# A new order table for a fused recurrence and feed-forward kernel

## The chip, the cores and the metric

The kernel runs on one core of a Trainium2 chip. The time is device microseconds of one execution; a profiled execution gives the trace. Engines are named as in the profile: PE (matmul), PEld (its weight loads), DVE (vector), ACT (activations), POOL, and SP, which here only issues DMAs.

## The reference

Four batches, eight heads, 768 steps, head size 48. A gated linear recurrence with a complex decay gives y, which is laid out as rows of 8 x 48 = 384 numbers; a layer norm and a two-layer network (384 to 1536 to 384) follow, with a residual.

```python
mag = np.sqrt(a_re * a_re + a_im * a_im)
scale = np.minimum(mag, 0.999) / (mag + 1e-06)
...
for t in range(S):
    new_re = ar * S_re - ai * S_im
    new_im = ar * S_im + ai * S_re
    kv = np.einsum('bhd,bhe->bhde', k[:, :, t], v[:, :, t])
    S_re, S_im = (new_re + kv, new_im)
    y[:, :, t] = np.einsum('bhd,bhde->bhe', q[:, :, t], S_re)
...
xn = (x - mu) / np.sqrt(var + 1e-06) * g_ln
ch = np.maximum(xn @ w_ch1, 0.0) @ w_ch2
return (x + ch).astype(np.float32)
```

## The kernel before

The 4 x 768 rows are 24 chunks of 128 steps, n = 0 to 23, taken as 12 pairs, P = 0 to 11 (three pairs in a batch). The recurrence is done chunk by chunk as masked attention: with cumulated log decays and phases, q and k are scaled so that a product of the two gives the weights inside a chunk, and a carried state G (384 numbers on each partition) brings in the past.

Every piece of work is an operation with a name. `name.P` and `name.P.i` belong to a pair, `name.n` to a chunk. Pair 0 is cut in two halves by heads (`.0.0` and `.0.1`), the others are whole. In the order of a pair:

- Inputs, by SP: `are`, `aim` (384 KB a pair, halves of 192 KB in pair 0), `k`, `q`, `vf` (192 KB a chunk).
- The decay: `ln`, `iv` (ACT), `r` = aim/are, `r2` = its square, `u` = log(1 + r2) (ACT), `l` and `lc` (DVE): the capped log of the magnitude. `dec` (PE) cumulates it with a triangular matrix, `e` and `en` (ACT) are its exponentials.
- The phase: `th` (arctangent, ACT), `ph` (PE) cumulates it, `car` carries its end to the next pair, `sin` and `cos` (ACT). In pairs 0 to 3 a small matmul `qt` adds a quarter turn in PSUM ahead of `cos`; it waits for `sin` and `car`. Later pairs take `abs` and a bias.
- `ke`, `qe` = k, q times the exponentials, `ks`, `qs` = those times cos and sin, on DVE or POOL. `v` is a cast of `vf`.
- Transposes: `kT`, `qT` on PE (eight 128-wide ones each) with the copies `ksT`, `qsT` on ACT or DVE, or `ksT`, `qsT` as a DMA transpose on SP, with no PE work.
- Attention: `am` (PE), `atm` (mask, DVE), `y` (PE, from `atm`, `v`, `qsT` and the state), `x` (copy). State: `gm` (PE), `G` (copy, or product with `decc`, which comes from `dps`).
- Network: `bn`, `rstd` (statistics), `xtr`, `xT` (x transposed), `mm1` (six groups of six matmuls a pair, three of `relu`), `mm2` (three groups of four a chunk), `ot` (scaling by rstd and residual; some are split into `oa` on ACT and `ot` on POOL), `st` (store, SP).

The layer norm's gain and mean are folded into w1 once: `wl.0` (POOL) loads w1 by DMA with a cast, `wp.0` to `wp.2` (PE) form its weighted column means, nine `wc` (DVE) subtract them; `mm1.P.g` needs `wc.g.*`. `wl.1` loads w2, which `mm2` needs.

Nothing is scheduled by the compiler. `PLAN` is a list of `name:engine`, with the PSUM bank behind the letter (`P0` is PE into bank 0, `A2` ACT reading bank 2), and its order is the order on each engine; `@other` makes the operation wait for another one too. An engine goes strictly through its list and waits for semaphores of others. Buffers are rings (`RINGS`); the order must respect them. Two kinds of entries compute nothing: `tab.log` and `tab.trig` (ACT) load the table of logarithm and exponential, or of sine and arctangent, ahead of their use; `warm` (PE) are fillers, matmuls whose result is not read, to keep TensorE busy while it would wait.

Of the kernel before, what the change touches and what calls it, by code (L numbers as in the profile page):

```python
# [806 lines left out]
```

## Time and profile before

| What | before |
|---|---|
| median of 3 runs | 193.94 us (193.87 to 194.18) |
| profiled execution | span 191.74 us, 193.94 us with what lies around the span |
| PE busy | 175.3 us (91%) |
| ACT busy | 165.2 us (86%) |
| DVE busy | 154.8 us (81%) |
| POOL busy | 109.2 us (57%) |
| table loads, fillers | 23, 74 |
| loads and stores | 37.56 MB, 196 GB/s over the span |

A busy share is an average over stages: in the first 37 us the engines wait for each other and for the inputs, later several are full at once. The page's fourth part, the chain, follows the end of the program back through what released each step. A matmul's duration in the trace includes its way through the array, which overlaps the next ones; what it costs in a dense run is the distance between starts.

### The profile page before, as it was taken

Reading aid. Unit: us, or ns where it says so; the run is one execution under the profiler, and the core shown is the slowest. Engines: PE = TensorE matmul, PEld = TensorE weight load, DVE = VectorE, ACT = ScalarE, POOL = GpSimd, SP = SyncE. Lnnn points to the kernel's source line nnn. Section 1 sums busy time; section 2 is a strip of 40 time slices with the busy share of each in tenths; the row PEclk is TensorE's granted clock in tenths of the full one; section 3 lists DMA queues with packets and bytes.
Section 4 is the critical chain, followed back from the end, with each engine's and each line's share of the span. In section 5 each row is a group of like instructions: output and inputs, shape, how many; then the busy total and the mean of one; then the engine's idle time right before and its main releaser. Section 6 shows DMA issues by size and latency. Waiting matters only on the chain.

```text
span 191.7 us, 5125 instructions
## 1 busy us (share of the span) xinstructions
PE 175.3 (91%) x2039; PEld 132.7 (69%) x2039; DVE 154.8 (81%) x267; ACT 165.2 (86%) x234; POOL 109.2 (57%) x124
## 2 busy tenths in 40 slices
PE   5567958999999989999999999999999999999991
PEld 3355644577786777787686877868777678787760
DVE  2369996999999998799999989997987484868612
ACT  3999999989999999999799988999999989427540
POOL 8601449927695599652496764585495857600500
PEclk9999996999999999999999999999999999999997
DMA  6999999999899979999899996999998979996033
GB/s 151 291 244 219 236 190 203 168 218 298 184 212 237 166 163 255 192 258 211 161 169 265 167 255 152 184 288 253 204 228 153 208 145 144 248 103 165 3 129 118
DMA packets 132104, 37.56 MB, mean 196 GB/s; under 512 B 127088, under 2 KB 131696, under 8 KB 132080
## 3 DMA queue, kind: packets, MB, share of 16 engines
q1 hardware_dynamic: 130128, 34.88, 87.7%
q0 software_dynamic: 1952, 2.36, 7.3%
q8 instruction: 16, 0.26, 0.5%
q14 instruction: 8, 0.07, 0.1%
HBM read 28.31 MB, written 4.72 MB: 172 GB/s over the span
## 4 chain that ended last, share of the span: by engine, by line
PE 38%; ACT 27%; DVE 16%; issue 8%; DMA 4%; POOL 3%; SPq 1%; DVEq 0%; POOLq 0%; ACTq 0%
PE banks L741 14%; PE banks L720 9%; ACT h L731 5%; ACT L775 4%; DVE w1b L388 3%; DMA qsT<-qs 3%; PE banks L477 2%; PE banks L616 2%; DVE l L466 2%; ACT r L462 2%; ACT en L481 2%; PE banks L496 2%; PE banks L593 2%; ACT r L458 2%; DMA are<-in_a_re_dram 2%
## 5 line engine op out<-in xcount | busy, mean ns | idle before, releaser
L741 PE MATMUL banks<-w2b,h 128*128 128x384 bf16 x288 | 54.9, 326 | 0.3 <-ACT h L731 0.2
L720 PE MATMUL banks<-xT,w1b 128*128 128x256 bf16 x432 | 51.9, 272 | 0.8 <-ACT trig L514 0.5
L720 PEld LDWEIGHTS <-w1b 128*128 128x128 bf16 x432 | 41.2, 98 | 7.7 <-DVE xT L291 1.3
L741 PEld LDWEIGHTS <-h 128*128 128x128 bf16 x288 | 26.0, 97 | 14.3 <-ACT h L731 0.8
L294 DVE TENSOR_TENSOR atm<-banks,mask 128x1024 bf16<-128x1024 f32 x24 | 28.7, 1217 | 5.2 <-PE banks L616 2.8
L731 ACT ACTIVATE h<-banks 128x1024 bf16<-128x1024 f32 x24 | 24.1, 1023 | 8.7 <-PE banks L720 8.5
L775 ACT ACT_TABLE_LOAD x23 | 29.5, 1283 | 1.2 <-PEq L791 0.8
L294 POOL TENSOR_TENSOR ks<-ke,trig 128x768 bf16<-128x768 bf16 x14 | 22.8, 1640 | 8.8 <-DVE ke L294 2.8
L294 POOL TENSOR_TENSOR qs<-qe,trig 128x768 bf16<-128x768 bf16 x11 | 18.0, 1641 | 12.3 <-DVE ot L755 5.0
L294 POOL TENSOR_TENSOR ke<-k,en 128x384 bf16<-128x384 f32 x18 | 16.5, 930 | 11.8 <-DMA vf<-in_v_dram 10.3
L294 POOL TENSOR_TENSOR qe<-q,e 128x384 bf16<-128x384 f32 x16 | 14.6, 921 | 12.2 <-ACT e L481 5.9
L733 DVE TENSOR_SCALAR h<-banks 128x1024 bf16<-128x1024 f32 x12 | 14.5, 1215 | 4.9 <-PE banks L720 4.9
L753 POOL TENSOR_TENSOR ot<-ot,x 128x384 f32<-128x384 f32 x8 | 7.3, 916 | 14.6 <-ACT ot L746 13.6
L616 PE MATMUL banks<-qsT,ksT 128*128 128x128 bf16 x192 | 14.3, 219 | 1.4 <-DVE ksT L291 1.2
L616 PEld LDWEIGHTS <-ksT 128*128 128x128 bf16 x192 | 12.1, 98 | 3.4 <-DVE ksT L291 1.4
L496 PE MATMUL banks<-th,u_th 128*128 128x384 f16 (+1 forms) x52 | 12.4, 325 | 2.2 <-ACT th L485 2.2
L679 DVE BATCH_NORM_STATS2 stats<-x 128x6 f32<-128x384 bf16 x24 | 13.1, 547 | 0.0
L755 DVE SCALAR_TENSOR_TENSOR ot<-banks,rstd,x 128x384 f32<-128x384 f32 x16 | 9.6, 609 | 4.1 <-DMA out_dram<-ot 2.9
L466 DVE SCALAR_TENSOR_TENSOR l<-r,w 128x768 f16<-128x768 f16 (+1 forms) x13 | 11.5, 892 | 1.6 <-ACT r L462 1.6
L770 PE MATMUL banks<-u_e 128*128 128x256 f16 x74 | 10.5, 302 | 2.2 <-POOL u_e L328 2.2
L477 PE MATMUL banks<-l,u_e 128*128 128x384 f16 (+1 forms) x52 | 10.4, 327 | 2.2 <-DVE l L469 1.3
L448 ACT ACTIVATE w<-are 128x768 f32<-128x768 f32 (+1 forms) x13 | 10.3, 796 | 2.2 <-DMA are<-in_a_re_dram 2.2
(96 smaller groups left out, 372.1 us busy)
## 6 DMA issues: line engine op xcount, KB each, us to landing
q<-in_q_dram SPq DMA_DIRECT2D x24, 192.0 KB, 4.0
k<-in_k_dram SPq DMA_DIRECT2D x24, 192.0 KB, 4.1
vf<-in_v_dram SPq DMA_DIRECT2D x24, 192.0 KB, 4.2
...
w2b<-in_moe_w_ch_dram POOLq DMA_DIRECT2D x1, 1152.0 KB, 11.9
```

The costliest lines, as they stand in the source:

```text
L294: {"DVE": nc.vector, "POOL": nc.gpsimd}[eng(name)].tensor_tensor(**kw)
L466: nc.vector.scalar_tensor_tensor(out=S_("l"), in0=S_("r2"), scalar=0.5, in1=S_("w"), op0=ALU.mult, op1=ALU.add)
L477: nc.tensor.matmul(heads(ps[:, c]), lhsT=u_e[:, c, j], rhs=step(T("l", P), j), start=(j == 0), stop=(j == R - 1))
L496: nc.tensor.matmul(heads(ps[:, c]), lhsT=u_th[:, c, j], rhs=step(T("th", P), j), start=False, stop=(j == R - 1), skip_group_check=True)
L616: nc.tensor.matmul(ps[:, h], lhsT=T("ksT", n)[:, h], rhs=T("qsT", n)[:, h], start=True, stop=True)
L679: nc.vector.bn_stats(out=T("stats", n), in_=T("x", n))
L720: nc.tensor.matmul(ps[:, jj], lhsT=w1b[:, dc, ts(gi * JG + jj, C)], rhs=T("xT", P)[:, dc].rearrange("p c t -> p (c t)"), start=(dc == 0), ...
L731: act(out=dst, in_=src, func=AF.Relu)
L733: nc.vector.tensor_scalar(out=dst, in0=src, scalar1=0.0, scalar2=None, op0=ALU.max)
L741: nc.tensor.matmul(bank(f"o.{n}")[:, 0:DM], lhsT=T("h", P)[:, j, ts(c, C)], rhs=w2b[:, j], start=(j == 0), stop=(j == NJ - 1))
L770: g.add(f"warm.{i}", lambda i=i: nc.tensor.matmul(bank(f"warm.{i}")[:, 0:256], lhsT=u_e[:, 0, 0], rhs=u_e[:, 1].rearrange("p j t -> p (j t ...
L775: g.add(f"tab.{nm}.{i}", lambda tab=tab: nc.scalar.preload_act_table_set(tab))
```

## The change

The whole order table is replaced, and the loop that declares fillers goes from 240 to 61. The operations that compute are the same; what differs is order, engine and bank, and which transposes are done by DMA. Counts in the table:

| kind | before | after |
|---|---|---|
| table loads (ACT) | 23 | 17 |
| fillers (PE) | 74 | 61 |
| kT and qT (PE) | 10 + 13 | 14 + 11 |
| ksT and qsT by DMA (SP) | 14 + 11 | 10 + 13 |
| ksT, qsT copies on ACT / DVE | 6 / 17 | 5 / 20 |
| ks, qs on POOL / DVE | 25 / 27 | 21 / 31 |
| ke, qe on POOL / DVE | 34 / 14 | 34 / 14 |
| xT on ACT / DVE | 11 / 13 | 7 / 17 |
| relu on ACT / DVE | 24 / 12 | 26 / 10 |
| G on ACT / DVE | 6 / 14 | 9 / 11 |
| r2 on ACT / DVE / POOL | 8 / 4 / 1 | 6 / 7 / 0 |
| v on ACT / DVE / POOL | 3 / 1 / 8 | 5 / 2 / 5 |
| rstd on ACT / POOL | 7 / 5 | 4 / 8 |

Up to the first mm1 the new table has 6 table loads, the old one 8. w1's load (`wl.0`) stood on POOL behind `v.0`; it now stands behind the constants and waits for `lc.0.1` on DVE. The inputs of pairs 0 and 1 come in another order on SP, `aim` first and `vf` last; pair 1's operations stand beside pair 0's, and pair 1's attention (`am.2`, `am.3`) ahead of the first mm1. The diff, cut to both tables' openings and ends:

```diff
@@ the order table @@
 PLAN = """
-are.1.0:S tab.log.0:A ln.1.0:A iv.1.0:A ue:G car0.1:G pad.ks.2:G zdec:G ident:G pad.ks.1:G pad.qs.0:G
-are.0.0:S gln:S are.0.1:S qrow:G car0.0:G pad.ks.0:G pad.qs.1:G ln.0.0:A pick:G iv.0.0:A ln.0.1:A aim.0.1:S
-aim.0.0:S uth:V iv.0.1:A r.0.1:V tab.trig.0:A th.0.1:A aim.1.0:S are.2.0:S q.0.0:S aim.2.0:S k.0.0:S q.2.1:S
-q.0.1:S k.0.1:S warm.0:P1 warm.1:P1 warm.2:P1 warm.3:P1 warm.4:P1 warm.5:P1 warm.6:P1 warm.7:P1 warm.8:P1
-warm.9:P1 warm.10:P1 warm.11:P1 warm.12:P1 warm.13:P1 warm.14:P1 warm.15:P1 warm.16:P1 warm.17:P1 warm.18:P1
-warm.19:P1 warm.20:P1 warm.21:P1 warm.22:P1 warm.23:P1 warm.24:P1 warm.25:P1 warm.26:P1 warm.27:P1
-warm.28:P1 ph.0.1:P0 q.1.0:S vf.0.1:S k.1.1:S r.0.0:V r2.0.0:A th.0.0:A one:G cmean:G wgc:V vf.0.0:S
-are.3.0:S sin.0.1:A0 k.1.0:S aim.3.0:S r2.0.1:V r.1.0:V r2.1.0:V tab.log.1:A u.0.0:A l.0.0:V u.0.1:A l.0.1:V
-lc.0.0:V warm.29:P2 warm.30:P2 warm.31:P2 warm.32:P2 warm.33:P2 warm.34:P2 warm.35:P2 warm.36:P2 warm.37:P2
-warm.38:P2 warm.39:P2 warm.40:P2 warm.41:P2 warm.42:P2 warm.43:P2 warm.44:P2 warm.45:P2 warm.46:P2
-warm.47:P2 warm.48:P2 warm.49:P2 warm.50:P2 warm.51:P2 dec.0.0:P1 u.1.0:A ln.2.0:A iv.2.0:A en.0.0:A1
-lc.0.1:V l.1.0:V dec.0.1:P2 ph.0.0:P3 car.0.1:V0 en.0.1:A2 e.0.1:A2 e.0.0:A1 lc.1.0:V r.2.0:V car.0.0:V3
-tab.trig.1:A sin.0.0:A3 qe.0.1.0:V qe.0.0.0:V q.1.1:S mask:G ke.0.0.0:G@qe.0.0.0 ke.0.1.0:V r2.2.0:V
-qs.0.0.1:V qs.0.1.1:V th.1.0:A qt.0.1:P0 warm.52:P4 warm.53:P4 warm.54:P4 warm.55:P4 warm.56:P4 warm.57:P4
-warm.58:P4 warm.59:P4 warm.60:P4 warm.61:P4 warm.62:P4 warm.63:P4 warm.64:P4 warm.65:P4 warm.66:P4
-warm.67:P4 warm.68:P4 warm.69:P4 qt.0.0:P3 dps.0:P2 cos.0.0:A3 cos.0.1:A0 ks.0.0.1:V ks.0.0.0:V ks.0.1.0:V
-qs.0.1.0:V ph.1.0:P4 dec.1.0:P6 qs.0.0.0:V warm.70:P1 warm.71:P1 qT.1:P3 tab.log.2:A en.1.0:A6 u.2.0:A
-ln.3.0:A iv.3.0:A e.1.0:A6 v.0:G@qs.0.0.0 decc.0:V2 ks.0.1.1:V vf.1.1:S vf.1.0:S q.2.0:S car.1.0:V4
-warm.72:P1 warm.73:P1 kT.0:P2 qT.0:P1 kT.1:P0 qsT.1:V3 tab.trig.2:A sin.1.0:A4 ksT.0:V2 wl.0:G ksT.1:V0
-am.1:P2 gm.0:P0 ke.1.0.1:G@ks.0.1.1 ke.1.0.0:G th.2.0:A qsT.0:V1 am.0:P6 dps.1:P1 decc.1:A1 qt.1.0:P4
-l.2.0:V r.3.0:V lc.2.0:V G.0:V0 gm.1:P0 cos.1.0:A4 dec.2.0:P4 k.2.1:S tab.log.3:A e.2.0:A4 en.2.0:A4
-atm.0:V6 atm.1:V2 G.1:V0 r2.3.0:V k.2.0:S are.4.0:S ph.2.0:P6 y.1:P1 aim.4.0:S ks.1.0.1:G@lc.2.0 x.1:V1
-are.5.0:S ks.1.0.0:G y.0:P2 kT.3:P3 x.0:V2 ksT.3:V3 u.3.0:A tab.trig.3:A sin.2.0:A6 wp.2:P0 wc.2.1:V0
-wc.2.0:V0 xtr.0:P1 wl.1:G xtr.1:P4 wp.0:P5 wp.1:P2 wc.2.2:V0 xT.1:V4 qt.2.0:P6 xT.0:A1 kT.2:P3 th.3.0:A
-cos.2.0:A6 wc.0.2:V5 wc.0.1:V5 wc.1.2:V2 wc.0.0:V5 wc.1.1:V2 ksT.2:A3 mm1.0.2.1:P0 mm1.0.2.0:P0
-qe.1.0.0:G@r2.3.0 qe.1.0.1:G qs.1.0.0:G relu.0.2:A0 ph.3.0:P6 qs.1.0.1:G qe.2.0.1:G qT.2:P3 qT.3:P4
-car.3.0:A6 mm1.0.0.1:P0 mm1.0.0.0:P0 wc.1.0:V2 qsT.3:V4 sin.3.0:A6 qt.3.0:P6 qsT.2:A3 mm1.0.1.0:P4 l.3.0:V
-lc.3.0:V qe.2.0.0:V aim.5.0:S v.1:G pad.qs.2:G am.3:P2 mm1.0.1.1:P4 cos.3.0:A6 bn.0:V bn.1:V relu.0.0:A0
-qs.2.0.0:G@qe.2.0.0 k.3.0:S q.3.1:S relu.0.1:A4 gm.2:P6 rstd.0:G am.2:P0 mm2.0.0:P7 dec.3.0:P4 G.2:A6
...
-st.19:S oa.18:A6 xT.22:V0 ot.18:G st.18:S mm1.11.0.0:P2 mm1.11.0.1:P2 mm1.11.1.0:P0 mm1.11.2.0:P6
-mm1.11.1.1:P0 bn.22:V relu.11.1:A0 mm1.11.2.1:P6 relu.11.0:V2 mm2.23.0:P5 mm2.22.0:P2 mm2.22.1:P2
-mm2.23.1:P5 ot.21:V4 st.21:S rstd.11:A relu.11.2:A6 mm2.22.2:P2 ot.22:V2 st.22:S mm2.23.2:P5 ot.23:V5
-st.23:S
+ue:G are.1.0:S are.0.0:S are.0.1:S aim.0.0:S pad.ks.1:G warm.0:P0 warm.1:P0 aim.0.1:S warm.2:P0 zdec:G
+pad.qs.1:G warm.3:P0 warm.4:P0 aim.1.0:S pad.ks.0:G warm.5:P0 warm.6:P0 warm.7:P0 one:G cmean:G warm.8:P0
+tab.log.0:A ln.1.0:A pad.qs.0:G warm.9:P0 warm.10:P0 aim.2.0:S qrow:G warm.11:P0 ln.0.0:A warm.12:P0 car0.1:G
+warm.13:P0 warm.14:P0 iv.0.0:A car0.0:G warm.15:P0 warm.16:P0 pad.qs.2:G k.0.1:S ln.0.1:A warm.17:P0
+warm.18:P0 pick:G warm.19:P0 iv.0.1:A r.0.0:V warm.20:P0 q.1.0:S iv.1.0:A warm.21:P0 warm.22:P0 r2.0.0:V
+warm.23:P0 r.0.1:V warm.24:P0 u.0.0:A warm.25:P0 q.0.1:S warm.26:P0 r2.0.1:V warm.27:P0 uth:V u.0.1:A
+warm.28:P0 r.1.0:V warm.29:P0 gln:S warm.30:P0 warm.31:P0 warm.32:P0 r2.1.0:V warm.33:P0 warm.34:P0 are.2.0:S
+warm.35:P0 warm.36:P0 l.0.0:V warm.37:P0 warm.38:P0 tab.trig.1:A th.0.1:A warm.39:P1 lc.0.0:V th.1.0:A
+ph.0.1:P0 k.0.0:S dec.0.0:P1 th.0.0:A car.0.1:V0 l.0.1:V sin.0.1:A0 q.0.0:S ph.0.0:P2 warm.40:P3 warm.41:P3
+car.0.0:V2 q.1.1:S wgc:V ph.1.0:P4 lc.0.1:V tab.log.2:A u.1.0:A k.1.1:S wl.0:G@lc.0.1 dec.0.1:P3 car.1.0:V4
+qt.0.1:P0 ln.2.0:A vf.0.0:S l.1.0:V warm.42:P6 ident:G warm.43:P6 warm.44:P6 warm.45:P6 e.0.0:A1 warm.46:P6
+warm.47:P6 vf.0.1:S iv.2.0:A warm.48:P6 lc.1.0:V dec.1.0:P6 en.0.1:A3 r.2.0:V k.1.0:S en.0.0:A1 e.1.0:A6
+are.3.0:S r2.2.0:V e.0.1:A3 qe.1.0.0:V u.2.0:A dps.0:P1 ke.0.0.0:V qe.0.0.0:V warm.49:P3 warm.50:P3 l.2.0:V
+warm.51:P3 warm.52:P3 warm.53:P3 warm.54:P3 warm.55:P3 warm.56:P3 qe.0.1.0:V warm.57:P3 warm.58:P3
+tab.trig.3:A sin.0.0:A2 ke.0.1.0:V cos.0.1:A0 qt.0.0:P2 lc.2.0:V sin.1.0:A4 warm.59:P3 qs.0.0.1:V warm.60:P3
+ks.0.0.1:V cos.0.0:A2 ks.0.1.0:V qt.1.0:P4 qs.0.1.1:V th.2.0:A ks.0.1.1:V dps.1:P0 ks.0.0.0:V cos.1.0:A4
+kT.1:P2 decc.1:V0 qs.0.1.0:V kT.0:P0 qs.0.0.0:V ksT.1:V2 qT.0:P3 qe.1.0.1:G@qs.0.0.0 qT.1:P4 qsT.0:V3 mask:G
+aim.3.0:S tab.log.4:A en.1.0:A6 wp.0:P5 decc.0:V1 qs.1.0.1:V qsT.1:A4 dec.2.0:P2 qs.1.0.0:V vf.1.1:S wc.0.0:V5
+ke.1.0.1:G@qs.1.0.0 ksT.0:A0 am.1:P6 wc.0.1:V5 qT.3:P4 vf.1.0:S ke.1.0.0:G e.2.0:A2 wc.0.2:V5 am.0:P0
+en.2.0:A2 v.0:G q.2.1:S qsT.3:V4 ks.1.0.0:V ln.3.0:A gm.0:P2 q.2.0:S ph.2.0:P4 atm.1:V6 ks.1.0.1:G@ks.1.0.0
+G.0:A2 iv.3.0:A k.2.0:S gm.1:P2 qT.2:P3 atm.0:V0 y.1:P6 r.3.0:G k.2.1:S kT.3:P7 G.1:V2 wp.1:P0 qsT.2:V3
+tab.trig.5:A sin.2.0:A4 are.4.0:S y.0:P1 kT.2:P2 ksT.3:V7 x.0:A1 v.1:G qt.2.0:P4 th.3.0:A ksT.2:V2 xtr.0:P7
+aim.4.0:S wl.1:G gm.2:P1 wc.1.0:V0 x.1:A6 ph.3.0:P2 G.2:A1 wc.1.1:V0 qe.2.0.0:G cos.2.0:A4 xtr.1:P6 wc.1.2:V0
+gm.3:P1 xT.0:A7 qe.2.0.1:G am.3:P4 sin.3.0:A2 xT.1:V6 wp.2:P0 atm.3:V4 qs.2.0.0:G car.3.0:A2 am.2:P6 qt.3.0:P2
+atm.2:V6 mm1.0.0.0:P4 cos.3.0:A2 qs.2.0.1:G mm1.0.0.1:P4 G.3:V1 y.3:P2 wc.2.2:V0 relu.0.0:A4 y.2:P1 x.3:V2
+pad.ks.2:G mm1.0.1.1:P6 x.2:A1 wc.2.0:V0 ke.2.0.0:G xtr.3:P2 r2.3.0:A mm1.0.1.0:P6 wc.2.1:V0 ke.2.0.1:G
+xT.3:A2 xtr.2:P1 qT.5:P3 bn.1:V xT.2:A1 qT.4:P4 ks.2.0.1:G qsT.5:V3 mm1.1.1.1:P0 qsT.4:V4 vf.2.1:S
+mm1.1.1.0:P0 bn.0:V tab.log.6:A u.3.0:A mm1.0.2.0:P2 ks.2.0.0:G are.5.0:S relu.0.1:V6 relu.1.1:A0 mm1.0.2.1:P2
+mm1.1.0.1:P4 bn.3:V ln.4.0:A vf.2.0:S mm1.1.0.0:P4 k.3.1:S kT.4:P0 relu.1.0:A4 mm1.1.2.0:P6 ksT.4:V0 k.3.0:S
+mm1.1.2.1:P6 iv.4.0:A l.3.0:V kT.5:P0 relu.0.2:A2 aim.5.0:S am.4:P4 lc.3.0:V ksT.5:V0 mm2.0.0:P1
...
+bn.20:V mm1.11.0.0:P4 bn.23:V mm1.11.0.1:P4 mm1.11.1.1:P6 relu.11.0:A4 mm1.11.2.0:P0 rstd.10:A mm1.11.1.0:P6
+oa.21:A2 ot.20:V3 mm1.11.2.1:P0 relu.11.1:A6 bn.22:V ot.21:G mm2.22.0:P2 relu.11.2:A0 mm2.23.0:P4 st.21:S
+st.20:S mm2.22.1:P2 rstd.11:A st.19:S mm2.23.1:P4 mm2.23.2:P4 mm2.22.2:P2 ot.23:V4 ot.22:V2 st.23:S st.22:S
 """
@@ the declared fillers @@
-    for i in range(240):
+    for i in range(61):
             bank(f"warm.{i}")[:, 0:256], lhsT=u_e[:, 0, 0], rhs=u_e[:, 1].rearrange(
```

## Prediction

> **What bounds the kernel now.** I read the table of stages first, then the groups kept apart by shape, the view of the tile w1b, and the chain that ended last. The columns of the stages: stretch, its length, busy time (count) of PE, PE's weight loads, DVE, ACT and POOL, granted clock, DMA share, GB/s.
>
> ```profile
> 15.00:19.20 4.20, 2.94 (x28) 2.18 (x26) 4.07 (x9) 4.17 (x8) 0.82 (x1) 1.00 1.08 222
> 25.30:28.80 3.50, 2.25 (x50) 1.86 (x51) 3.50 (x7) 3.46 (x6) 0.78 (x2) 1.00 1.04 188
> 28.80:32.20 3.40, 2.52 (x14) 1.19 (x11) 3.10 (x4) 3.13 (x5) 3.40 (x3) 0.58 1.09 209
> 37.40:50.00 12.60, 12.35 (x155) 9.70 (x156) 12.36 (x21) 11.63 (x16) 6.16 (x9) 1.00 1.12 233
> 110.00:140.00 30.00, 29.72 (x361) 23.17 (x360) 27.23 (x47) 28.03 (x39) 17.62 (x17) 1.00 1.01 226
> 165.00:187.70 22.70, 22.52 (x241) 16.72 (x239) 14.46 (x27) 10.29 (x19) 3.76 (x5) 1.00 0.61 125
> 187.70:191.80 4.10, 0.00 (x0) 0.00 (x0) 0.64 (x2) 0.00 (x0) 0.00 (x0) 0.75 0.27 98
> ```
>
> From 37.4 us to 187.7 PE is never idle for long; before that ACT and DVE are full and PE waits or runs fillers. After 165 only PE is full. So the time is: when PE gets into its dense run, how much PE work is left then, and 4.05 us of tail (last store).
>
> ```profile
> L775 ACT ACT_TABLE_LOAD x23 | 29.5, 1283 | 1.2 <-PEq L791 0.8
> L593 PE MATMUL banks<-ident,qs 128*128 128x128 bf16 x104 | 7.8, 219 | 0.1
> ```
>
> ```profile
> L720 PE MATMUL banks<-xT,w1b x432: 269/272/283, 37.4 to 183.5; 128*128 128x256 bf16 x144
> DMA to landing us min/median/max: 9.9/9.9/9.9
> ```
>
> The dense run begins with the first mm1, at 37.4. The other line is w1's load; POOL issues it at 22.7, so it lands at 32.6, and the first wp, its first reader, starts at 33.9.
>
> ```profile
> 6.93 0.42 ACT w L448
> 7.37 0.52 ACT are L450
> 7.91 1.28 ACT L775
> 9.21 0.52 ACT th L485
> ...
> 29.82 1.44 PE banks L477 x4
> ...
> 76.65 0.65 PE banks L477 x4
> ...
> 95.38 3.93 PE banks L720 x36
> ...
> 100.32 0.45 PE banks L616 x8
> ...
> 183.79 3.92 PE banks L741 x24
> ```
>
> In the chain the reader sees PE's true prices, since a group's mean of one matmul (326 ns) overlaps its neighbours: a whole mm1 of a pair takes 3.93 us (36 matmuls), a whole mm2 of two chunks 3.92 (24), dec 0.65, eight 128-wide matmuls (am, kT, qT) 0.45. At 29.82 the same dec takes 1.44, at the granted clock of 0.58.
>
> **A balance of PE.** With such spacings from start to start (ph 0.97, y 0.41, gm 0.20 or 0.37 with the carried state, xtr 0.17, dps 0.29, wp 0.65, qt 0.43, pair 0's halves dec 0.33, ph 0.80, qt 0.25) all PE work without fillers is 159.6 us. Of it 14.5 lie ahead of the first mm1 and 145.1 behind. The dense run lasts 187.7 - 37.45 = 150.2, so 5.1 us of it are small gaps. The span of 191.74 has 2.2 us around it: the profiled execution is 193.94, which is the median of the runs.
>
> **The change, part by part.**
>
> *Six table loads fewer.* One costs 1283 ns, and the chain shows nothing more: the activation before it ends at 7.89, it runs 7.91 to 9.19, the next starts at 9.21. 6 x 1.29 = 7.7 us off ACT. Moves to and from ACT at its row means (start to start 0.37 for a copy, 0.9 for a relu or a ksT copy: G +3, relu +2, v +2, x +1, car +2, abs +1, qsT +1, xT -4, r2 -2, rstd -3, decc -2, ksT -2) add about 1.0. ACT falls from 160.2 to 153.5 us by those spacings. That is worth nothing by itself, since PE is the bound behind 37.4; it counts as cover there and directly in the opening. The Trainium skill, "ScalarE: Activation LUTs", What ACT_TABLE_LOAD costs, puts a drain of about 1380 ns on each switch, 2.66 us in all: by it ACT would lose 16 us instead of 7.7. The trace disagrees, with 1.32 us between two activations around a load, and the sum goes by the trace.
>
> *Two more transposes on PE.* 25 groups of eight instead of 23: + 2 x 0.45 = 0.9 us of PE work, none of it hidden. The two DMA transposes that go (25 to 23 on SP) save nothing that PE waits for there; the two copies out of PSUM that replace them are in the sums here. DVE goes from 149.4 to 149.6, POOL falls by about 6 us (ks 14 to 9 at 1.64, v 8 to 5 at 0.83, against rstd +3 at 0.93, qs, r and the halves): neither is a bound.
>
> *Fillers.* 74 to 61, at 0.11 us. They stand where PE waits for ACT or DVE in both tables, so: nothing.
>
> *w1's load.* It now waits for lc.0.1 on DVE and is issued at about 14 us, not 22.7. SP has sent the same number of bytes by then as before (17 loads, four of 384 KB), the 17th of which landed at 18.1. In before, vf.1.0 (issued 21.9) and w1 landed together at 32.6, 7.4 us after the load ahead of them, while a 192 KB load otherwise adds 0.85. I take the same 7.4: w1 lands at 18.1 + 7.4 = 25.5, and vf.0.1 with it. Everything queued behind on SP is pushed back: k.1.0 to 26.4, are.3.0 to 27.8, aim.3.0 to 29.1, vf.1 to 30.8. Who needs them: wp.0 (PE) when qT.1 is done, about 25.3; ke.1.0.0 (POOL) at 27.7; ln.3 (ACT) at 29.1; r.3 (POOL) at 31.8. All just in time. Bounds: not sharing with inputs at all, 14.1 + 9.9 = 24; sharing evenly with SP's loads, about 29. I take 25.5, by the nearest row. Behind wp.0 in PE's order stand dec.2, am.1, qT.3, am.0: a late w1 holds pair 0's attention too, and DVE's three wc.
>
> *Pair 1 beside pair 0.* This is where the time comes from. The new order runs pair 1's phases, decays and trig beside pair 0's, with 6 table loads ahead of the first mm1 and not 8. ACT's list up to car.3, which the last qt ahead of the first mm1 waits for: 5 loads after the first (6.4 us), 16 half activations of pair 0 at 0.43 (6.9), 20 whole ones of pairs 1 to 3 at 0.75 (15.0), ksT and qsT (1.8), five small copies and car (2.3): 32.4. It starts when are.1.0 lands, 4.24 as before (first on SP in both). Waits that I find by following it: about 0.9 (u.0.0 on DVE's r2, x.0 on y.0, sin.3 on ph.3). So car.3 ends at 37.5, qt.3 takes 0.5, and the first mm1 starts at 38.0. DVE, followed the same way, has atm.1 and atm.0 at 30.1 to 32.4, the three ksT/qsT at 32.9 to 34.9, wc.1 to 36.8 and xT.1 at 37.2: it just fits. Bounds for the first mm1: 37.1 (ACT waits for nothing) and 41 (w1 lands at 29).
>
> So the first mm1 is 0.55 us *later*. But PE has more behind it then: ph.3, qt.3, two more transposes, am.2, am.3, gm.2, gm.3: 0.97 + 0.43 + 0.9 + 0.9 + 0.57 = 3.8. Work behind the first mm1: 145.1 + 0.9 - 3.8 = 142.2.
>
> *Right behind the first mm1.* qT.5, kT.4 and kT.5 need POOL's chain v.1, w2's load, two qe, two qs, two ke, two ks: by its row means from 33.6 it gives qs.2 at 40.5 and ks.2 at 46.1; PE, with 0.65 a half mm1, reaches qT.5 at 41.5 and kT.4 at 46.5. It fits by 0.4 us. w2, issued at 34.4 with a landing time of 11.9, is there at 46.3; the first mm2 comes at 49.2.
>
> **Sum.** 193.94 + 0.55 (first mm1) - 2.9 (142.2 against 145.1), small gaps and tail as before (the last two stores stand in the other order at the same distance): 191.6. The gaps of 5.1 us should shrink a little, since ACT, full until 145 us, has 6.7 us less to do: between 0 and 3, I take 0.6, near the lower end, as PE also waited for orders of its own. A half-clock window in the opening, below, may cost up to 1.7 against one that cost about 1.6 in before, in dec.2 (1.23 for 0.65, start to start) and ph.2 (1.81 for 0.97): no difference taken. Forecast 191.0.
>
> **Rivals.**
>
> *More: ACT's slack closes the gaps.* Of the 5.1 us, 3 or more go. For it: ACT is 92% busy or more in each of the stages from 37 to 165 in before, and in the list of waits PE's weight loads and matmuls wait for its relu, trig and copies. Against: each such wait is 0.1 to 0.5 us, and DVE has no slack to give. 188.0 to 189.5. Chance 0.2.
>
> *Nothing comes of it: the lead is given back.* POOL's ks.2 or the copies of pairs 2 and 3 come 2 to 3 us late, and PE, now 3.3 us further on, meets them as idle time: 193 to 195. For it: the fit of 0.4 us above. Against: by sums of work up to each relu, ACT's pairs 3 to 9 are ready 5 to 8 us sooner than before. Chance 0.13, a fifth of it within 0.2%.
>
> *Slower: w1 collides with pair 1's inputs.* w1 shares evenly with SP's loads, lands at 29 or later, and k.1.0 with it. wp.0 holds PE, the three wc hold DVE, and the first mm1 moves from 38.0 by what exceeds 26. It decides when w1 lands behind 28.9, where the gain of 2.9 is gone; at 30.5, 195.6. For it: DMA share is 1.0 or more from 2 us on, so nothing is free. Against: in before w1 got through nearly undivided. The Trainium skill, "DMA: Bandwidth & Descriptors", Queues, rings and completion order, has each DMA engine go round robin between its queues packet by packet, which speaks for this rival; the 9.9 us of w1 in before, with SP's loads outstanding all the while, show a share of most of the engines. Chance 0.1.
>
> *Half clock where it hurts.* From about 14 to 23 us PE has some 4 us of work in the new order, and the half clock was granted in before behind a stretch with 2.25 of 3.5 busy. The Trainium skill, "TensorE: Matmul & The Clock Gate", Part 1, lets one idle window of about 3.4 us halve the clock, and fewer fillers make that likelier; before's single stretch of 3.4 us agrees in length, though PE was not idle ahead of it. If a second such stretch falls on transposes of pairs 0 and 1, DVE's chain moves by 1 to 2: 192 to 193. Chance 0.12, counted as faster.
>
> **How the numbers follow.** The forecast's own case (190 to 192) has 0.45. Less than 0.2% either way, 0.4 us, is what a measurement here cannot tell from no change. Faster: 0.45 + 0.2 + 0.12 = 0.77; the same 0.03; slower 0.1 + 0.1 = 0.2. The range leaves out the best of the first rival and the worst of the slower ones: 188.8 to 194.9.
>
> **What would show it.** 17 table loads, ACT busy near 158; w1 issued at 14 and landing near 25.5; the first mm1 at 38 (37 to 39) with am.3 and gm.3 ahead of it; PE's last matmul near 185; at most 5 us of small gaps in between. Wrong if w1 lands behind 28, if the first mm1 starts behind 41, or if PE idles over 8 us behind it.

## The result, and the profile after

The changed kernel takes 194.40 us (median of 15 runs, 193.68 to 195.84), the kernel before 193.94 us in the same comparison (15 runs, 193.37 to 194.82). The ratio is 1.0033, with a 95% interval of 1.0018 to 1.0049: slightly slower, and on the other side of the forecast of 191.0. In this document "after" is the changed kernel and "before" the old one. In the experiments the medians hold every execution, but the ratios leave out the slow ones, among them one of a_fill (its profiled one, 364 us) and one of b_w1 (358 us) that went at half TensorE speed from end to end.

The profiled execution of after took 194.84 us with a span of 193.1. From its page, the span, the table loads and am (L611):

```profile
span 193.1 us, 5126 instructions
L770 ACT ACT_TABLE_LOAD x17 | 21.8, 1283 | 1.1 <-PEq L786 0.8
L611 PE MATMUL banks<-qsT,ksT 128*128 128x128 bf16 x192 | 14.6, 219 | 1.7 <-DMA qsT<-qs 1.7
```

From the view of the tile w1b in after: mm1 (the two numbers ahead of the semicolon are the first and the last start), and w1's landing.

```profile
L715 PE MATMUL banks<-xT,w1b x432: 269/273/283, 39.8 to 184.7; 128*128 128x256 bf16 x144
DMA to landing us min/median/max: 11.1/11.1/11.1
```

The table of stages of after (columns as before: stretch, length, busy time of PE, its weight loads, DVE, ACT and POOL, granted clock, DMA share, GB/s):

```profile
24.00:27.40 3.40, 3.40 (x33) 3.22 (x31) 2.38 (x7) 2.63 (x4) 1.35 (x3) 0.50 0.89 174
...
50.00:80.00 30.00, 30.00 (x353) 22.65 (x352) 26.65 (x49) 29.68 (x41) 14.37 (x17) 1.00 0.98 220
80.00:110.00 30.00, 29.56 (x373) 22.91 (x372) 28.16 (x47) 28.62 (x40) 23.15 (x21) 1.00 0.95 195
110.00:140.00 30.00, 29.10 (x348) 21.79 (x347) 26.37 (x49) 25.96 (x36) 15.06 (x15) 1.00 0.97 202
140.00:165.00 25.00, 22.60 (x263) 17.05 (x261) 18.66 (x37) 19.53 (x27) 14.23 (x12) 1.00 1.03 169
```

The last of these stages in before:

```profile
140.00:165.00 25.00, 24.72 (x283) 18.65 (x281) 16.73 (x29) 23.20 (x32) 18.59 (x17) 1.00 0.97 173
```

And from the chain of after, the stretch of that last stage in which PE waits:

```profile
154.29 0.88 POOL qe L289
155.18 1.02 SPq L593
...
156.87 1.77 SPq L593
158.75 4.99 DMA qsT<-qs
163.88 0.61 PE banks L611 x8
```

The reader sees three things. The first mm1 is at 39.8, not 38.0. The half clock has moved from dec.2 and ph.2 (28.8 to 32.2 in before) to the transposes of pair 0 (24.0 to 27.4), where PE does twice the time for the same work. And late in the run, where before was full (24.72 of 25 us), PE has idle time: am.20 waits 1.27 us and am.19 0.75, each for a DMA transpose (the last one lands 5 us after its issue). Waits and gaps of PE are taken here from start to start, less the usual distance; the profile counts idle time alone, so its rows are a little lower (1.7 us for these two).

From the two traces, by the balance of the prediction:

| Term | forecast | measured |
|---|---|---|
| first mm1 (before 37.45) | +0.55 | +2.34 |
| PE work behind it (before 145.28) | -2.9 | -2.86 |
| small gaps behind it (before 4.96) | -0.6 | +1.7 |
| tail (before 4.05) | 0 | +0.2 |
| around the span (before 2.20) | 0 | -0.46 |
| sum | -2.95 | +0.9 |

The second and third row split the dense run (150.2 us in before, 149.1 in after) by the spacings of the prediction, so the split is an estimate; by PE's busy time in that stretch (148.4 and 145.3 us) it is -3.1 and +1.9. Either way the work moved as forecast. What ate it is the opening (1.8 us more than forecast) and, as the largest term, the gaps (2.3 us more).

### The profile page after: what moved, and what is told of

The parts are those of the page before. It is cut to its first block, busy times and chain, and to the rows that moved or that the text cites. A ratio compares the mean times of both kernels' runs of the same rounds, so it can differ in the third digit from the quotient of the medians.

```text
span 193.1 us, 5126 instructions
## 1 busy us (share of the span) xinstructions
PE 175.3 (91%) x2042; PEld 133.6 (69%) x2042; DVE 151.7 (79%) x276; ACT 159.4 (83%) x222; POOL 104.8 (54%) x123
## 4 chain that ended last, share of the span: by engine, by line
PE 52%; DVE 17%; ACT 12%; DMA 7%; SPq 4%; issue 4%; POOL 2%; DVEq 0%; ACTq 0%
PE banks L736 16%; PE banks L715 15%; PE banks L588 5%; PE banks L611 3%; DMA qsT<-qs 3%; DMA aim<-in_a_im_dram 2%; SPq L593 2%; PE banks L491 2%; ACT L770 2%; DVE l L461 2%; DMA k<-in_k_dram 2%; ACT trig L509 2%; ACT th L480 2%; PE banks L661 2%; PE banks L682 2%
## 5 line engine op out<-in xcount | busy, mean ns | idle before, releaser
L715 PE MATMUL banks<-xT,w1b 128*128 128x256 bf16 x432 | 51.3, 273 | 0.0
L726 ACT ACTIVATE h<-banks 128x1024 bf16<-128x1024 f32 x26 | 26.3, 1020 | 5.4 <-PE banks L715 5.2
L289 POOL TENSOR_TENSOR qe<-q,e 128x384 bf16<-128x384 f32 x18 | 16.4, 917 | 22.8 <-DVE qs L289 8.4
L289 POOL TENSOR_TENSOR qs<-qe,trig 128x768 bf16<-128x768 bf16 x12 | 19.6, 1641 | 7.7 <-DVE ks L289 5.5
L289 POOL TENSOR_TENSOR ke<-k,en 128x384 bf16<-128x384 f32 x16 | 14.5, 916 | 9.9 <-DVE l L464 5.6
L289 POOL TENSOR_TENSOR ks<-ke,trig 128x768 bf16<-128x768 bf16 x9 | 14.7, 1642 | 7.7 <-DVE ks L289 6.8
L611 PE MATMUL banks<-qsT,ksT 128*128 128x128 bf16 x192 | 14.6, 219 | 1.7 <-DMA qsT<-qs 1.7
L728 DVE TENSOR_SCALAR h<-banks 128x1024 bf16<-128x1024 f32 x10 | 12.1, 1214 | 4.9 <-PE banks L715 4.9
L611 PEld LDWEIGHTS <-ksT 128*128 128x128 bf16 x192 | 12.0, 97 | 4.0 <-issue 2.6
L491 PE MATMUL banks<-th,u_th 128*128 128x384 f16 (+1 forms) x52 | 11.9, 313 | 2.5 <-ACT th L480 2.5
L289 POOL TENSOR_TENSOR r<-aim,are 128x768 f16<-128x768 f32 x6 | 10.9, 1817 | 4.1 <-ACT are L445 4.1
L457 ACT ACTIVATE r<-r,one_b 128x768 f16<-128x768 f16 (+1 forms) x13 | 11.5, 887 | 0.7 <-DVE r L289 0.6
```

The costliest lines, as they stand in the source:

```text
L289: {"DVE": nc.vector, "POOL": nc.gpsimd}[eng(name)].tensor_tensor(**kw)
L457: add(f"u.{X}", lambda S_=S_: act(out=S_("r2"), in_=S_("r2"), func=AF.Ln, bias=one_b), needs=[f"r2.{X}", "one"], uses=[("r2", P)])
L491: nc.tensor.matmul(heads(ps[:, c]), lhsT=u_th[:, c, j], rhs=step(T("th", P), j), start=False, stop=(j == R - 1), skip_group_check=True)
L611: nc.tensor.matmul(ps[:, h], lhsT=T("ksT", n)[:, h], rhs=T("qsT", n)[:, h], start=True, stop=True)
L715: nc.tensor.matmul(ps[:, jj], lhsT=w1b[:, dc, ts(gi * JG + jj, C)], rhs=T("xT", P)[:, dc].rearrange("p c t -> p (c t)"), start=(dc == 0), ...
L726: act(out=dst, in_=src, func=AF.Relu)
```

## The experiments

Times are medians, ratios are to before, each with runs of before on the same chip. The clock rows come from the profiled executions.

| Run | what | us | ratio, 95% interval |
|---|---|---|---|
| a_fill | after, 32 fillers more | 193.55 | 0.9962 [0.9938, 0.9987] |
| a_qT | after, two DMA transposes by PE | 194.69 | 1.0045 [1.0022, 1.0068] |
| a_loads | after, six loads of the table in force | 194.18 | 1.0021 [1.0001, 1.0040] |
| b_w1 | before, w1 early | 198.07 | 1.0202 [1.0177, 1.0227] |
| a_warm | after, 42 fillers more | 194.09 | 1.0001 [0.9973, 1.0029] |
| a_best | a_warm, inputs reordered, two transposes by PE | 195.56 | 1.0083 [1.0060, 1.0106] |
| b_fill | before, 29 fillers more | 194.19 | 1.0004 [0.9984, 1.0025] |
| b_w1p | b_w1, one execution for its trace | 197.76 | |
| a_sw | after, six table switches more | 202.94 | 1.0469 [1.0432, 1.0505] |
| a_w1late | after, w1 4 us later | 197.68 | 1.0173 [1.0141, 1.0205] |
| a_full | after, 56 fillers more | 193.06 | 0.9962 [0.9946, 0.9977] |
| a_full2 | a_full, two transposes by PE | 192.78 | 0.9941 [0.9923, 0.9959] |
| a_open | after, one switch and back ahead of car.3 | 197.94 | 1.0191 [1.0160, 1.0223] |
| a_late | after, the late 26 of the 56 fillers | 192.62 | 0.9930 [0.9906, 0.9953] |
| a_early | after, the early 30 of the 56 fillers | 192.50 | 0.9939 [0.9915, 0.9962] |
| b_full | before, 46 fillers more | 193.13 | 0.9957 [0.9939, 0.9974] |
| a_bare | after, 21 fillers fewer | 194.69 | 1.0040 [1.0007, 1.0073] |

### Fillers, first try: a_fill, a_warm, b_fill

a_fill puts 32 fillers where PE idled between 12 and 25 us (the loop that declares them grows with them, here and below).

```diff
 warm.48:P6
+warm.61:P6 warm.62:P6 warm.63:P6 warm.64:P6 warm.65:P6 warm.66:P6
...
 warm.58:P3
+warm.67:P3 warm.68:P3 warm.69:P3 warm.70:P3 warm.71:P3 warm.72:P3
...
 warm.60:P3
+warm.85:P3 warm.86:P3 warm.87:P3 warm.88:P3 warm.89:P3
...
 dps.1:P0
+warm.90:P3 warm.91:P3 warm.92:P3
```

> The changed kernel with 32 more fillers (0.11 us each), in bank P6 behind warm.48 (6) and in P3 behind warm.58 (18), warm.60 (5) and dps.1 (3), all where TensorE waits for ScalarE or VectorE between 15 and 24 us. Theory (the half clock that falls on the transposes of pair 0, kT.1 to wp.0, holds up the first mm1): no stretch of half clock at 24 to 27.3 us, these transposes 0.45 us each instead of 0.85, the first mm1 at 38.3 to 38.8 instead of 39.8, the time 1.0 us below the changed kernel, so 0.2 to 0.4 % below the kernel before (193.4). Rival (ScalarE's own list sets the first mm1, the slow transposes lie beside it): the clock is full, the first mm1 stays within 0.3 us of 39.8, the time stays at 194.4 to 194.6.

a_warm has nearly the same (16 instead of 18 behind warm.58), and 3 more behind warm.41 and 9 ahead of dps.0.

```diff
 warm.41:P3
+warm.61:P3 warm.62:P3 warm.63:P3
...
 u.2.0:A
+warm.70:P1 warm.71:P1 warm.72:P1 warm.73:P1 warm.74:P1
...
 dps.0:P1
```

> The changed kernel with 42 more fillers in the places where TensorE waits between 13 and 24 us: 3 behind warm.41, 6 behind warm.48, 9 ahead of dps.0 (bank P1), 16 behind warm.58, 5 behind warm.60, 3 behind dps.1. Theory (half clock in the opening costs the changed kernel its lead): granted clock 0.99 or more, the first mm1 at 38.3 to 38.8 us, the time 192.0 to 193.0, so 0.5 to 1.0 % below the kernel before. Rival (the clock is not what delays it): 194.2 to 194.8.

b_fill does the like in before, ahead of dec.0.0, qt.0.0 and am.1.

```diff
 warm.51:P2
+warm.80:P2 warm.81:P2 warm.82:P2 warm.83:P2 warm.84:P2 warm.85:P2
...
 warm.69:P4
+warm.91:P4 warm.92:P4 warm.93:P4 warm.94:P4 warm.95:P4 warm.96:P4
...
 ksT.1:V0
+warm.100:P3 warm.101:P3 warm.102:P3 warm.103:P3 warm.104:P3
```

> The kernel before with 29 more fillers where TensorE waits ahead of its own half clock (28.8 to 32.2 us): 11 behind warm.51, 9 behind warm.69, 9 ahead of am.1. Theory (the half clock there costs dec.2 and ph.2 1.6 us and the later fillers are too few or too early to prevent it in each execution): 192.8 to 193.9, gain 0 to 1.1 us. Rival (fillers are as good a remedy here as in the changed kernel): 192.4 or less.

a_fill is below before, a_warm equals it, though it has more fillers. The single runs say why: those of a_warm with a mean granted clock of 0.994 or more took 192.3 to 193.4, the others (0.986 to 0.991) 193.9 to 195.5. The cover was not complete, and some runs still met a half-clock stretch. The mean clock sorts the runs of a_warm, but not those of after: there 0.991 went with 195.0 and 195.6, 0.978 to 0.980 with 194.2 to 195.1, 0.988 with 193.7 and 194.0. So what a stretch costs depends on what it falls on. In b_fill's profile two such stretches are left in the opening (10.4 and 30.9 us), so it decides nothing about before.

### Fillers, second try: a_full, a_early, a_late, a_bare, b_full

a_full has 15 fillers ahead of ph.0.1 (8 to 10 us), 6 behind warm.48, 9 ahead of dps.0, 18 behind warm.58, 5 behind warm.60 and 3 behind dps.1. a_early is the first three groups, a_late the last three.

```diff
 th.1.0:A
+warm.61:P0 warm.62:P0 warm.63:P0 warm.64:P0 warm.65:P0 warm.66:P0
...
 ph.0.1:P0
...
 u.2.0:A
+warm.82:P1 warm.83:P1 warm.84:P1 warm.85:P1 warm.86:P1 warm.87:P1
...
 dps.0:P1
```

> After with 56 more fillers (15 ahead of ph.0.1, 6 behind warm.48, 9 ahead of dps.0, 18 behind warm.58, 5 behind warm.60, 3 behind dps.1), so that PE has work wherever it idles from 8 to 25 us. Theory (half clock on pair 0's transposes costs 1.3 us of the first mm1): first mm1 at 38.5, span 190.7, time 192.4 to 193.2, faster than both. Rival (which 3.4 us stretch is slow depends on the run, whatever PE does; fillers stand in the way): 194 to 195, with a half-clock stretch in the opening all the same.

> After with only the early 30 of the 56 fillers (8 to 17 us). Theory (the gain is at the transposes, 24 to 27 us): 194 to 194.6. Rival (it is in ph, dec and car before 18 us): 193.0 to 193.4. If neither alone gains, the half clock only moves from one place to the other.

> After with only the late 26 of the 56 fillers (18 to 25 us, ahead of and between pair 0's transposes). Theory (the gain of 1.4 us is half clock on the transposes and the copies behind them, 24 to 27 us): 193.0 to 193.4, a half-clock stretch before 18 us harmless. Rival (the gain is in the stretches before 18 us, where ph, dec and car are PE's and other engines wait for them): 194 to 194.6.

Both halves gain by themselves, 1.9 and 1.8 us against after by the medians, which neither expectation had: what counts is not one place. With a_full, whose profile has no half clock from 7 us up to its last microseconds, all twelve runs lie between 192.76 and 194.08, so more fillers than either half bring nothing more. Its first mm1 is not at the expected 38.5 but where it is in after (from its tile view, and ACT's groups from 24 to 40 us):

```profile
L721 PE MATMUL banks<-xT,w1b x432: 269/273/283, 39.9 to 183.2; 128*128 128x256 bf16 x144
L449 ACT ACTIVATE w<-are 128x768 f32<-128x768 f32 x1 | 0.8, 843 | 0.5 <-DMA are<-in_a_re_dram 0.5
```

ACT does not wait for pair 0's transposes there, but it comes to them 0.4 us later than in after and then waits 0.5 us for are.3.0. What the profiled a_full gains on the profiled after (1.5 us) lies behind the first mm1, in a dense run of 147.5 us instead of 149.1. The stage from 24.0 us in a_early, from its table of stages, with the first mm1 and the landing of the late qsT transposes (140 to 166 us) from its tile views:

```profile
24.00:27.40 3.40, 3.04 (x37) 2.18 (x36) 3.29 (x9) 3.37 (x5) 1.36 (x4) 1.00 1.08 218
...
140.00:165.00 25.00, 24.24 (x295) 18.37 (x294) 19.65 (x36) 20.14 (x27) 14.06 (x13) 1.00 0.96 180
```

```profile
L718 PE MATMUL banks<-xT,w1b x432: 269/273/282, 38.6 to 181.5; 128*128 128x256 bf16 x144
```

```profile
DMA to landing us min/median/max: 3.1/3.5/3.9
```

The same row of after's tile view, over 140 to 170:

```profile
DMA to landing us min/median/max: 4.3/4.8/5.0
```

So the profiled a_early (191.69 us, below its median) has the first mm1 1.2 us sooner and 1.8 us less gaps (4.82, against 6.65) than the profiled after. How the clock gets into ACT's list shows in the groups of ACT between 24 us and about the first mm1, first of after and then of a_early (busy us and mean ns, then idle before and the releaser):

```profile
L284 ACT COPY qsT<-banks 128x1024 bf16<-128x1024 bf16 x1 | 1.0, 1012 | 0.7 <-PE banks L588 0.7
```

```profile
L287 ACT COPY qsT<-banks 128x1024 bf16<-128x1024 bf16 x1 | 1.0, 1007 | 0.0
```

ACT waits 0.74 us for kT.1, kT.0, qT.0 and qT.1, which take 0.85 each at half clock and 0.45 at full. The wait is 0.74 to 0.89 us in the seven profiles where such a stretch lies on these transposes (after, a_loads, a_bare, a_open, a_qT, a_sw, a_w1late), and none above 0.12 in those of a_early, a_late, a_warm, a_full and a_full2. That is the direct price of the half clock here; of the other 0.4 us between after and a_early, 0.25 were there before, when ACT began en.1.0 (25.75 and 25.50 us).

b_full adds 8 fillers ahead of dps.1 and 9 ahead of dec.2 to b_fill.

```diff
 am.0:P6
+warm.120:P1 warm.121:P1 warm.122:P1 warm.123:P1
...
 cos.1.0:A4
+warm.128:P1 warm.129:P1 warm.130:P1 warm.131:P1
```

> Before with 46 more fillers where PE idles ahead of dec.0, qt.0.0, am.1, dps.1 and dec.2. Theory (the new order is worth something once both have cover): no half clock in the opening, 192.8 to 193.6, not below a_full's 193.06. Rival (the order is worth nothing or less): 192.0 to 192.7, below it.

Before gains too, 0.8 us. In its profile (194.13) one stretch, at 9.6 us, is left, and the first mm1 is at 37.4 as in before. Between b_full (0.9957) and the covered versions of the new order (0.9930 to 0.9962) the intervals overlap: by the medians the new order with cover is 0.1 (a_full) to 0.6 us (a_early) ahead, and that it is ahead at all is not shown.

a_bare goes the other way and takes warm.40 to warm.60 out of after.

```diff
-warm.40:P3 warm.41:P3
...
-warm.42:P6
...
-warm.57:P3 warm.58:P3
...
-warm.59:P3
...
-warm.60:P3
```

> After without the last 21 of its 61 fillers (warm.40 to warm.60, about 12 to 24 us). Theory (the more PE idles ahead of the transposes, the more of the opening runs at half clock, and the later the first mm1): half-clock stretches of 7 us or more in the opening, first mm1 at 40 to 41, time 195 to 196.5. Rival (after's fillers already do nothing, and the gain of the added ones came from something else): 194.0 to 194.8.

Its median is only 0.3 us above after's, within the intervals and in the range of the rival: the dose is not shown in this direction. Its profile has 6.8 us of half clock, twice after's, and the first mm1 at 39.7, as in after. Its runs spread further (193.23 to 196.14), and they go with the clock: 193.2 to 193.7 at 0.973 to 0.981, 194.6 and 194.7 at 0.970, 195.0 to 196.1 at 0.955 to 0.964. Its table of stages shows what goes ahead of a half-clock stretch:

```profile
17.20:20.60 3.40, 0.78 (x18) 0.44 (x17) 3.37 (x6) 3.38 (x6) 0.00 (x0) 1.00 1.06 191
20.60:24.00 3.40, 1.98 (x24) 1.10 (x24) 3.21 (x12) 3.39 (x7) 0.00 (x0) 0.50 1.08 206
24.00:27.40 3.40, 3.40 (x32) 3.17 (x30) 2.35 (x8) 2.48 (x4) 1.35 (x3) 0.50 0.92 177
```

A window of 3.4 us with PE busy for 0.78 is followed by half clock, and a window that is itself slow and busy for 1.98 by another. In after it took less idleness (PE alone, its busy time behind the length):

```profile
17.20:20.60 3.40, 2.16 (x29) 1.00 1.03 171
20.60:24.00 3.40, 1.60 (x26) 1.00 1.07 204
24.00:27.40 3.40, 3.40 (x33) 0.50 0.89 174
```

Here 2.16 of 3.4 us kept the clock and 1.60 lost it. The line is not quite sharp, as a window of before and one of a_late show:

```profile
25.90:29.30 3.40, 2.01 (x47) 1.53 (x45) 3.40 (x6) 3.35 (x6) 1.06 (x1) 1.00 1.04 194
```

```profile
9.50:12.90 3.40, 1.79 (x17) 1.45 (x17) 2.61 (x7) 3.37 (x6) 0.00 (x0) 1.00 0.91 171
```

Before lost the clock behind 2.01, a_late kept it behind 1.79. Taken along the edges of such windows, from the first record of the clock (5.4 to 8.2 us) on and without the tail, all traces at hand say this: behind each of the 16 windows with PE busy for 1.78 of 3.41 us or less the clock was halved, behind none with more than 2.01; in between it was halved behind two (before, a_open) and kept behind twelve. The Trainium skill, "TensorE: Matmul & The Clock Gate", Part 1, has the clock halved after an idle window of about 3.4 us. The length agrees: each stretch in these traces is a multiple of 3.41 us (3.4, 6.8, 10.2, 13.7), or cut off by the end. "Idle" does not: PE was busy for 47% of the window in after, and for 59% in before.

### The late transposes: a_qT, a_full2, a_best

a_qT makes qsT.19 and qsT.20 by PE and a DVE copy right ahead of their readers.

```diff
-qsT.19:S
...
+qT.19:P1 qsT.19:V1
 gm.18:P3
...
-qsT.20:S
...
+qT.20:P3 qsT.20:V3
 am.20:P2
```

> The changed kernel with qsT.19 and qsT.20 transposed on TensorE (qT.19, qT.20, copies on VectorE) instead of by DMA. Theory (the gaps of 0.75 us ahead of am.19 and 1.27 us ahead of am.20 come from the 4 to 5 us that a DMA transpose takes to land): both gaps go, TensorE has 0.9 us more to do, the time is 0.9 to 1.1 us below the changed kernel (193.4). Rival (qs.9 and qs.10 themselves come late, behind sin.11, ks.10 and qe.10 on GpSimd): the waits stay under other names, the time is 194.4 to 195.3.

The waits came back under another name: am.19 0.81 and am.20 1.0 us, now for DVE's copy. No gain. a_full2 puts them earlier, on top of a_full.

```diff
 ke.10.0.1:G
+qT.19:P3 qsT.19:V3
 ph.11.0:P4
...
 en.11.0:A6
+qT.20:P5 qsT.20:V5
 mm1.9.0.0:P2
```

> The same fillers, and qsT.19 and qsT.20 by TensorE and a DVE copy (qT.19 ahead of ph.11.0, qT.20 ahead of mm1.9.0.0) instead of by DMA. Theory (am.19 and am.20 waited 0.75 and 1.27 us for these two DMAs in after; 0.9 us of PE work is added, but lies in PE's other idle time at 144 and 152): 0.5 to 1 us below the kernel with the fillers alone, 191.8 to 192.5. Rival (the late one is DVE's or ACT's work for chunks 18 to 21, and the wait returns under another name): equal to it, or up to 0.9 us slower.

It takes 192.78 against 193.06, with overlapping intervals: neither the gain of the theory nor quite the rival. am.20's wait is gone, am.19 waits 0.51 for DVE, and 0.9 us of PE work is added; in a_full itself, with DMA transposes that landed faster, am.20 waited 0.17 only. a_best has these two and a_warm's fillers ("the run above" in its expectation is a_warm), and lets pair 0's halves load and start ahead of pair 1's.

```diff
-are.1.0:S
 are.0.0:S
...
 aim.0.1:S
+are.1.0:S
...
-ln.1.0:A
...
 iv.0.1:A
+ln.1.0:A
```

> The fillers of the run above; qT.19 and qT.20 on TensorE again, now with half a microsecond or more of TensorE work between each and its am, so that the copy lies beside it; and the inputs of pair 0's halves (are, aim) ahead of pair 1's are on SP, with ln.0 and iv.0 ahead of ln.1 on ScalarE. Theory: 0.5 us from an earlier start of ScalarE (first activation at 3.6 instead of 4.26), 1.0 us from the gaps at am.19 and am.20: 190.6 to 191.8. Rival (what is gained in the opening is lost again to waits behind 110 us, since the order there was made for another pace): 192.0 to 193.0, no better than the run above.

The reordering backfired: ACT starts 0.7 us sooner and then waits 2.2 us for are.1.0, which lands at 7.76; the first mm1 is at 41.4. A half-clock stretch at 12.9 was there as well. Its 195.56 lies above both expectations.

### w1's load: b_w1, b_w1p, a_w1late

One part of the change alone: in before, w1 is issued behind lc.0.1.

```diff
 lc.0.1:V
+wl.0:G@lc.0.1
...
-wl.0:G
```

> The kernel before with one part of the change alone: w1's load is issued by GpSimd as soon as lc.0.1 is done (14.3 us) instead of behind v.0 (22.7 us). Theory (an early w1 is of use only in an order that reads it early; here it only pushes vf.0, k.1 and pair 2's loads back by some 7 us, and v.0, gm.0, y.1 with them): w1 lands near 25, the first mm1 not earlier than 37.4 and up to 2 us later, the time 194 to 196. Rival (w1's landing at 32.6 us, just ahead of the first wp, sets the first mm1): first mm1 1 us or more earlier, 193.0 or less.

> The kernel before with w1's load behind lc.0.1, once more for its trace. Theory: w1 lands near 25 us; vf.0.0, k.1.0 and are.3 land 6 to 8 us later than in before, v.0 and gm.0 with them, or ScalarE waits for ln.3; the first mm1 some 3 us later than 37.4. Rival: the inputs land as before and the 4 us are lost behind the first mm1.

It costs 4 us, more than the theory allowed. In the profile w1 is issued at 14.9 and lands 10.4 us later; are.3.0 lands at 27.85, not 21.2, and ACT waits for it (its groups between 20 and 42 us):

```profile
L445 ACT ACTIVATE w<-are 128x768 f32<-128x768 f32 x1 | 0.8, 843 | 4.0 <-DMA are<-in_a_re_dram 4.0
```

The first mm1 is at 41.7, the gaps behind it are before's. In after are.3.0 lands even later (29.3), but the new order puts ln.3 behind pair 1's work, and it starts at 30.5 without a wait: the early w1 is affordable with that order. And there it must be early:

```diff
-wl.0:G@lc.0.1
...
 r2.2.0:V
+wl.0:G@r2.2.0
```

> After, with w1's load issued behind r2.2.0 instead of lc.0.1, about 4 us later (18.7 instead of 14.7). Theory (w1's landing sets wp.0, and wp.0 holds dec.2, am.1 and pair 0's attention behind it on PE): w1 lands at 29.5 to 30, wp.0 starts 2.5 to 3 us later than in after, the first mm1 at 41.5 to 42.5, 196 to 197. Rival (pair 1's inputs, which w1 pushed back by 7 us, set the opening): they land 3 to 4 us sooner, the first mm1 is at 39 to 40 and the time is 193.5 to 194.5.

The time rises by 3.3 us, somewhat more than the theory has. w1 lands at 30.0, wp.0 starts at 30.05 instead of 27.06, and the first mm1 at 43.9. PE's clock is halved as well, from 21.3 on, so how much of this is w1's alone is not shown (table of stages of a_w1late):

```profile
21.30:34.90 13.60, 9.98 (x81) 7.51 (x82) 7.90 (x22) 8.67 (x12) 3.92 (x6) 0.50 1.00 195
```

### ACT: a_loads, a_sw, a_open

a_loads repeats six loads right behind themselves.

```diff
 tab.log.6:A
+tab.log.20:A
...
 tab.trig.7:A
+tab.trig.21:A
```

> The changed kernel with six table loads doubled (the same table once more, behind loads 6 to 11, between 44 and 115 us): ScalarE gets back the 7.7 us that the change took off it. Theory (ScalarE's work is cover there, TensorE is the bound): 0 to 1.0 us more than the changed kernel (194.4 to 195.4). Rival (ScalarE is as much the bound as TensorE between 37 and 145 us): 4 us or more on top (198.4 or more).

Its trace has 17 loads: a load of the table in force does not run. So it is after once more (194.18), and says nothing on ACT. But it says something on the clock: its profile (193.98) has 10.2 us of half clock, from 18.4 on, three times after's, and the first mm1 at 39.5. The amount of half clock does not set the time. a_sw has six real switches, three times to the other table and back.

```diff
+tab.trig.20:A
 relu.1.1:A0
+tab.log.21:A
...
+tab.trig.22:A
 relu.3.1:A2
+tab.log.23:A
...
+tab.trig.24:A
 x.10:A1
+tab.log.25:A
```

> After, with six more table loads on ACT that really switch: three pairs (to the other table and back) around relu.1.1 (44 us), relu.3.1 (about 70 us) and x.10 (about 103 us), 6 x 1.29 = 7.7 us more of ACT, so that it is as full from 44 to 105 us as it can be. The forecast priced ACT's relief behind the first mm1 at 0.6 us in all, as cover for PE. Theory 'cover': PE stays the bound, ACT's queue of relu and copies runs later by 2.6 us at each place and catches up in its idle time (0.3 us between 50 and 80, 1.4 between 80 and 110, 4.0 between 110 and 140), so PE loses 1 to 3 us: 195.5 to 197.5. Rival 'ACT is level with PE there' (ACT busy 29.7 of 30 us from 50 to 80): nearly all of the 7.7 comes through on PE, 200 to 202. Rival 'nothing': 194.4, and the relief of the change was worth nothing.

The rival "level with PE" holds, and a little more: 8.5 us for 7.7 us of ACT. Its profiled execution took 204.21 and has the first mm1 1.5 us later than after's, ahead of all six switches; but the dense run alone, 156.9 us against 149.1, is 7.8 us longer, so what is added to ACT there comes through whole. PE's groups between 44 and 120 us wait for ACT; the table of stages of a_sw shows one place where the clock adds to it:

```profile
111.90:115.30 3.40, 1.29 (x16) 1.00 (x14) 2.92 (x6) 3.39 (x5) 1.03 (x2) 1.00 0.99 174
115.30:118.70 3.40, 3.40 (x23) 2.48 (x21) 1.20 (x2) 2.54 (x3) 3.40 (x4) 0.50 1.15 291
```

A wait of 2.27 us for ACT's en left PE with 1.29 busy, and the next 3.4 us ran at half clock, about 1.6 us more (18 matmuls of mm1 took 3.73 us, where half of the usual 3.93 is 1.97).

a_open adds one switch and back ahead of car.3.

```diff
+tab.log.20:A
 x.0:A1
+tab.trig.21:A
```

> After, with one pair of real table switches around x.0 on ACT (33 us), 2.6 us more of ACT's list ahead of car.3. Theory (the forecast's rule: ACT's list up to car.3 sets the first mm1): first mm1 2.6 us later, 42.4, and the time 194.4 + 2.6 = 197.0 (less a little that PE's gaps behind take up: 196.3 to 197.0). Rival (DVE's wc and xT, or POOL, set it): first mm1 at 39.8 to 40.8, 194.4 to 195.4.

ACT's list does delay the program: 3.1 us by the ratios for 2.6 us of ACT (3.5 by the medians), above the range of the theory and far from the rival. Its profiled execution took 200.16, so only its order of events is read: car.3 ends at 42.1, near the theory, but the first mm1 starts at 45.1. xtr.0 waits 1.0 us for x.0 and ph.3 1.3 us for th.3, and behind that the last work ahead of the first mm1 runs at half clock, so in this execution it is PE, not car.3, that comes last:

```profile
38.30:45.10 6.80, 5.87 (x37) 3.59 (x38) 2.17 (x3) 3.79 (x7) 5.05 (x6) 0.50 1.25 201
```

## Why the prediction was wrong

Right were the 17 loads and ACT's 159.4 us busy, w1's issue (14.74) and landing (25.8), that am.3 and gm.3 stand ahead of the first mm1, that w1 pushes are.3.0 back without holding ACT (it landed at 29.3, forecast 27.8), the work left behind the first mm1 (142.42 by the spacings), and the rule that ACT's list up to car.3 sets the first mm1: it starts 0.5 us behind car.3 in after and in every other profile of the new order but a_open's, where PE came last. The 194.40 lies inside the stated range, but that is luck: its upper part was kept for other causes, above all a late w1, which landed in time.

**The step that failed first: "Fillers. 74 to 61 ... so: nothing", with "no difference taken" for the half clock.** Fillers alone bring 1.8 to 1.9 us of the miss of 3.4 by the medians (a_early, a_late; 1.3 in a_full), so the term was not nothing. The rival "Half clock where it hurts" had the mechanism and the place, at a price of 1 to 2; but it was counted as faster, since the lead was taken as 2.9 in all. Half clock on the four transposes of pair 0 costs 0.74 to 0.89 us of ACT's list directly. The rest of what the fillers bring lies mostly behind the first mm1 (all of it in a_full's profile), and how they bring it there is not shown.

**Second, ACT's list was priced too low.** Followed from the start of ln.1.0 to the end of car.3 it takes 35.0 us in after: 33.3 of work (forecast 32.4) and 1.7 of waits (forecast 0.9). In a_early and a_late it takes 33.0 and 33.4 of work and 0.7 of waits. So 0.6 to 1.0 of the miss at the first mm1 is the sum of small durations, and about 0.8 the half clock.

**Third, "the gaps should shrink a little".** By size this is the largest term: -0.6 in the forecast, +1.7 in after's profile. The forecast read ACT's relief as cover from 37 to 165. a_sw shows that ACT is no cover up to 105 us: it is nearly as full as PE (29.68 and 28.62 of 30 us), and what is added there comes through whole. The relief shows up behind 110 (25.96 of 30 us, against 28.03), where PE's gaps have other causes: am.19 and am.20 (2.0 us together) wait for transposes whose qs come late from POOL, DVE and SP. In a_early and a_late, whose transposes landed sooner, the gaps are 4.8 and 4.7, near the 4.5 of the forecast. Put into the forecast's own sum, a_early's numbers (first mm1 at 38.59, gaps of 4.8 against the 5.1 that the prediction counted in before) give 193.94 + 1.14 - 2.9 - 0.3 = 191.9; that execution took 191.69, the median is 192.50. The balance closes, its inputs were wrong.

What stays open, and with it the cause of most of the gaps: why the transposes of chunks 18 to 20 land in 4.4 us (mean) in after and in 3.5 in a_early and a_late. In the five profiles (191.7 to 193.3 us) without half clock in the opening the mean is 3.5 to 3.8; in the twelve with one it is 3.3 to 4.6. That the clock and the landing are connected is not shown, and a_bare's profile (6.8 us of half clock, 3.3 us to land, 193.59) speaks against it.
